# Starting the form of 64 steps at unit 8 instead of unit 12 in an RWKV attention fused with a SwiGLU feed-forward

## The chip, the cores and the metric

The kernel runs on one core of a Trainium2 chip. A core has five engines with instruction streams of their own: TensorE (PE: matmuls, with weight loads shown as PEld), VectorE (DVE), ScalarE (ACT), GpSimd (POOL) and SyncE (SP), which here does nothing but issue DMAs. Each engine works through its stream in the order in which the program emits it, and semaphores make one engine wait for another. The metric is the device time of one execution in microseconds (us), as the median of several runs.

## The reference

A linear attention with a per-channel decay, over 4 batches, 8 heads, 768 steps and 48 channels a head, is followed by a SwiGLU feed-forward over its 3072 x 384 output:

```python
for t in range(S):
    kt, vt, rt = (k[:, :, t], v[:, :, t], r[:, :, t])
    cur = np.einsum('bhd,bhe->bhde', u[None] * kt, vt)
    y[:, :, t] = np.einsum('bhd,bhde->bhe', rt, state + cur)
    state = w[None, :, :, None] * state + np.einsum('bhd,bhe->bhde', kt, vt)
...
g = x @ w_gate                       # x: y as (3072, 384), w_gate: (384, 1536)
val = x @ w_val
return (g / (1 + np.exp(-g)) * val @ w_out)
```

## The kernel before

**Units.** The attention is cut into 24 units. A unit below `PAIRED` is 128 steps of one batch. A unit from `PAIRED` on is 64 steps of two batches: one batch in partitions 0 to 63, the other in 64 to 127 (`part`, `pieces_of`). The decay is folded into the keys and receptances (`scale_k`, `scale_r`, on GpSimd), so that inside a unit only a masked product is left.

**What a unit goes through.**

- `load` and `load_v` bring k, r and v in by SP's queue: three kinds of transfer, where a unit of two batches needs twice as many DMAs of half the size.
- `scale_k`, `scale_r`, and `own_product` (r times k times u, for the step's own term; `own_sum` adds it up on VectorE, `diagonal` lets ScalarE write it out as diagonal matrices).
- The turn, which puts channels on partitions. Below `BLOCKS` TensorE does it (`turn`: eight transposes by matmul, then two copies on ScalarE). From `BLOCKS` on, SP moves 32-wide blocks into one fixed pair of tiles (`move_blocks`: four DMAs, or eight for a unit of two batches) and VectorE transposes these 32 x 32 blocks (`turn_block` n = 0 for the keys, 1 for the receptances).
- `scores` (keys by receptances) and a masked copy of the scores into `At` on VectorE. For a unit of two batches, `fill_turned` (SP) and `fill_own` (ScalarE's queue) put the turned receptances and the diagonals into the other halves of `At`.
- `outputs` (TensorE; ScalarE copies the result into `xT`), and `update` or `paired_update` of the state (TensorE, VectorE, GpSimd). The last updates before `PAIRED` copy the state into the free half of `v_ld` by SP.

**The stages.** The loop over `s` is the pipeline. In stage `s` unit `s + 1` is scaled, unit `s` is turned, the scores of unit `s - 1` and the outputs of unit `s - 2` are computed. From `LATE` on, the outputs and the update of unit `s - 2` stand right behind the scores instead of at the end of the stage. Between these parts stand up to five gaps (`gaps(s, n)`). In stages 4 to 11 the table `EARLY` says what fills a gap: `R` is one step of the weights (`round_weights`, or later `weight_sum`), `F` is one `feed`.

**The weights.** The feed-forward's weights come as 64-bit numbers in 18 chunks: 0 to 11 for gate and value, 12 to 17 for the output matrix. One `R` rounds chunk n on ScalarE (`round_high`, `round_low`, `round_high`) and VectorE (`round_dve`), adds the low part of chunk n - 1 on GpSimd, and lets SP load chunk n + 2 (`load_weights`, into three buffers `w_bits`). In stage 7 chunks 10, 11 and 12 are rounded and 12, 13 and 14 loaded; in stage 8 chunks 13, 14 and 15 are rounded and 15, 16 and 17 loaded; in stage 9 chunks 16 and 17 are rounded.

**feed.** One `feed` takes the next item of the feed-forward from `todo` (for example `gate_value`: 12 matmul records into one of two PSUM banks, a Silu on ScalarE, a product on VectorE that gives the bank back), then one deferred piece of the attention's VectorE work from `lazy`, then one to three diagonals from `small`. `after_visit(s)`, in stages from `PAIRED` on, writes down the order of `lazy`: masked copies, `own_term` (`own_sum` and `diagonal` of the next unit), `turn_block(s, 0)`, a masked copy, `turn_second`, a masked copy, and the sums of the state. `turn_second` is more than VectorE's work:

```python
def turn_second():
    turn_block(s, 1)
    fill_turned(s)
    if s + 1 < N:
        scale_r(s + 1)
        move_blocks(s + 1)
        if s + 3 < N:
            load(s + 3)
```

What is left in `lazy` and `small` at the start of the next stage's scores is emitted there. From stage 12 on, a formula spreads the items left in `todo` over the gaps.

Of the kernel before, what the change touches and what calls it, by code (L numbers as in the profile page):

```python
# [22 lines left out]
def fast(  # L23
# [31 lines left out]
    N = B * NCH  # L55
# [64 lines left out]
    def rhat_of(i):  # L120
        return rhat[i % 2 if i < BLOCKS else i % 4 // 2]

# [3 lines left out]
            return khat[i][:, :, 0:D], rhat[i % 2][:, :, 0:D]  # L126
        return k_ld[i % 2][:], r_ld[i % 2][:]

    PAIRED = 12

    def part(i, p):

        c, q = divmod(i - PAIRED, 2)
        return 2 * q + p, PAIRED // B * P + 64 * c

    def pieces_of(i):

        if i < PAIRED:
            c, b = divmod(i, B)
# [3 lines left out]
    def load(i):  # L143
        for src, dst in zip((k, r), raw(i)):
            for rows, b, t in pieces_of(i):
                n = rows.stop - rows.start
                sp.dma_start(out=dst[rows], in_=src[b, :, t : t + n, :].rearrange("h t d -> t h d"))  # L147
# [106 lines left out]
    def round_weights():  # L254
        if done["act"] > done["pool"]:
            round_pool()
        round_act()
# [15 lines left out]
    def own_sum(i):  # L273
        dus[i] = three.tile([P, H], FP32, name="du", tag="du")
        dve.tensor_reduce(dus[i][:], rks.pop(i), axis=AX.X, op=ALU.add)
# [51 lines left out]
    for l in range(7):  # L327
        n = 1 << l
# [15 lines left out]
    def at(i, a):  # L344

        return HP - 1 - a if i >= BLOCKS and i % 2 else a

# [7 lines left out]
    def scale_r(i):  # L355
        pool.tensor_mul(rhat_of(i)[:, :, 0:D], raw(i)[1], rscale)
# [14 lines left out]
    def diagonal(i, on_act=None):  # L371

        du = dus.pop(i)
        if i >= PAIRED:
            small.extend(
                lambda h=h: act.activation(  # L376
                    own[:, i % 2, slot(i, h), :], ident64, AF.Identity, scale=du[:, h : h + 1]
                )
                for h in range(H)
            )  # L380
            return
        on_act = on_act or (HP if i < 4 else H)
        small.extend(
            lambda h=h: act.activation(
                At[i % 2][:, h, :], ident[:], AF.Identity, scale=du[:, h : h + 1]
            )
            for h in range(on_act)
        )
        if on_act < H:
            n = H - on_act  # L390
            pool.tensor_mul(
                At[i % 2][:, on_act:H], ident[:].unsqueeze(1).to_broadcast([P, n, P]),
                du[:, on_act:H].unsqueeze(2).to_broadcast([P, n, P]),
            )
# [16 lines left out]
    def move_blocks(i):  # L411


        h = hats[:].rearrange("p n h x -> p (n h x)")
        first, step = ((0, 1), (11, -1), (12, 1), (23, -1))[i % 4]
        if i < PAIRED:
            for m in range(4):
                src = h[:, P * first + 32 * m : P * first + 32 * m + 1]
                sp.dma_start(
                    out=h[32 * m : 32 * m + 32, 24 * P : 32 * P],  # L420
                    in_=bass.AP(
                        tensor=src.tensor, offset=src.offset,
                        ap=[list(src.ap[0]), [P * step, 2 * HP], [1, 32]],
                    ),
                )
            return
        first = 2 * first + (step < 0)
        for p in range(2):
            for n in range(2):
                for m in range(2):  # L430
                    q, o = 64 * p + 32 * n, 64 * first + 32 * m
                    src = h[q : q + 32, o : o + 1]
                    q, o = 64 * (1 - p) + 32 * m, 63 * 64 + 32 * n
                    dst = h[q : q + 32, o : o + 1]
                    sp.dma_start(
                        out=bass.AP(
                            tensor=dst.tensor, offset=dst.offset,
                            ap=[list(dst.ap[0]), [-64, 2 * H], [1, 32]],
                        ),
                        in_=bass.AP(  # L440
                            tensor=src.tensor, offset=src.offset,
                            ap=[list(src.ap[0]), [64 * step, 2 * H], [1, 32]],
                        ),
                    )

    def turn_block(i, n):

        if n == 0:
            turned[i] = three.tile([P, HP, P], FP32, name="rT", tag="rT")
        dst = (kT[i % 2], turned[i])[n]  # L450
        if i < PAIRED:
            merged = hats[:, 6:8].rearrange("p n h x -> p (n h x)").rearrange(
                "p (q n a x) -> p n q a x", q=4, n=2, a=HP
            )
            dve.transpose(dst[:].rearrange("p a (t q) -> p q a t", q=4), merged[:, n])
        else:
            dve.transpose(dst[:].rearrange("p a t -> p (a t)"), blocks[n])

    def after_visit(s):
# [10 lines that stand above are left out]
        def own_term():  # L470
            own_sum(s + 1)
            diagonal(s + 1)

        masked, sums = list(lazy)[:4], list(lazy)[4:]
        if len(masked) < 4:
            masked = [*masked, *(lambda: None for _ in range(4 - len(masked)))]
        lazy.clear()
        lazy.extend([
            *masked[:2], own_term if s + 1 < N else lambda: None,
            lambda: turn_block(s, 0), masked[2], turn_second, masked[3], *sums,  # L480
        ])

    lazy = deque()

    def scores(i):
# [20 lines left out]
        lazy.popleft()()  # L506
        if i < BLOCKS:
            lazy.popleft()()
# [10 lines left out]
    def fill_turned(i):  # L519

        rT = turned[i][:].rearrange("p a (e t) -> p (a e) t", e=2)
        for p in range(2):
            there = slice(64 - 64 * p, P - 64 * p)
            sp.dma_start(out=both(i)[there, p], in_=rT[there])
# [187 lines left out]
    def weight_sum():  # L712

        n = len(summed)
        o = (wt[1][:], w12, wt[0][:], wt[2][:])[n]
        a, b = ((w22, w12), (w12, w11), (w22, w12), (w21, wt[0][:]))[n]
        pool.tensor_sub(o, a, b)
        summed.append(n)
# [584 lines left out]
    summed = []  # L1303
    todo = []

    def feed(n, pops=1):
        for _ in range(n):
            ready = [k for k, (need, _) in enumerate(todo) if need <= done["pool"] + len(summed)]
            if ready:
                todo.pop(ready[0])[1]()  # L1310
            for _ in range(min(len(lazy), 1 + (len(lazy) > 9))):
                lazy.popleft()()
            for _ in range(min(pops, len(small))):
                small.popleft()()
# [22 lines left out]
    def gaps(s, n):  # L1337

        if s not in EARLY:
            if n == 0:  # L1340
                coming = 40 * ((s < 14) + (s < 18)) + 14 * (s < 22)
                share[0] = -(-(len(todo) + coming) // max(25 - s, 1))
            feed(
                share[0] // 5 + (n < share[0] % 5) - (n == 1 and BLOCKS <= s < PAIRED),
                1,
            )
            return
        for what in EARLY[s][n]:
            if what == "R":
                if done["pool"] < NW:  # L1350
                    round_weights()
                elif len(summed) < 4:
                    weight_sum()
            else:
                feed(1, 3)

    share = [0]
    BLOCKS = 10
    LATE = 12
    EARLY = {s: ("" if s < 7 else "R", "F", "R", "F", "RF") for s in range(5, 12)}  # L1360
    EARLY[4] = ("R", "F", "", "F", "F")

# [87 lines left out]
    for s in range(4, N + 2):  # L1450
        if 4 < s <= PAIRED:
            own_sum(s)
        if s == PAIRED:
            diagonal(s)
        late = BLOCKS < s + 1 < N and s % 2 == 0
        if s + 3 == PAIRED:

            for e in range(2):
# [3 lines left out]
                sp.dma_start(out=w64[rows, :, 1 - e], in_=w64[o : o + 64, :, 1 - e])  # L1462
        if s + 1 == BLOCKS:
            turn(s)
# [14 lines left out]
        if 4 <= s - 1 < N:  # L1479
            flush()  # L1480
            while lazy:
                lazy.popleft()()
            if s - 2 >= PAIRED:
                outputs(s - 2)
                if s < N:
                    fill_own(s)
            scores(s - 1)
            if LATE <= s < PAIRED + 2:
                outputs(s - 2)
                update(s - 2)  # L1490
                fill_own(s)
            if PAIRED <= s < N:
                load_v(s)
                after_visit(s)
            gaps(s, 1)
# [14 lines left out]
        gaps(s, 2)  # L1510
        if 4 <= s - 2 < LATE - 2:
            outputs(s - 2)
# [35 lines left out]
    n = nc.values_load(outside, min_val=0, max_val=512)  # L1548
# [416 lines left out]
```

## Time and profile before

| | |
|---|---|
| median of 3 runs | 581.66 us (581.47 to 581.78) |
| profiled execution | 582.02 us, its span 580.2 us |
| mean granted TensorE clock | 0.999 |
| DMA | 48.09 MB in 151734 packets, of them 139313 under 512 B |
| stage 8, from the scores of unit 7 to those of unit 8 | 74.80 to 86.95 us |
| stage 14, from the scores of unit 13 to those of unit 14 | 177.24 to 201.10 us |

The span runs from the first to the last instruction; the time of an execution lies a little around it. In the lines of the profile a row of the chain or of a timeline gives the start, the length, the engine, what it writes or the line of the kernel, and how many instructions are merged (x8). SPq and ACTq are the DMAs that SP and ACT issue. TensorE's fp32 matmuls show as two records each. The lines of the kernel that matter here: L405 the turn by TensorE, L494 scores of a 128-step unit, L645 its outputs, L658 its update; L546, L580 and L594 the same three for a unit of two batches; L688 `gate_value`; L204 and L210 the rounding on ACT; L219 and L220 on VectorE; L252 the addition on GpSimd; L184 the loading of a chunk; L147 `load`; L153 `load_v`; L419 and L435 `move_blocks`; L457 `turn_block`; L524 `fill_turned`; L530 `fill_own`; L675 the copies of the state; L384 and L376 the diagonals.

### The profile page before, as it was taken

The page shows a single profiled execution, that of the slowest core. Times are in us where ns is not written, and L with a number is a line of the kernel's source. Part 1 is how long each engine was busy: PE and PEld are TensorE (multiplying, and loading weights), DVE is VectorE, ACT ScalarE, POOL GpSimd, SP SyncE. Part 2 cuts the span into 40 slices and gives each one's busy share as a digit, 9 for nine tenths or more (in the row PEclk, how much of TensorE's full clock was granted, in tenths as well). Part 3 has the DMA queues.
Part 4 walks back from the last instruction along what each step waited for, and adds up shares of the span by engine and source line. Part 5 has one row for each costly group of instructions (what it writes and reads, how often), then busy time and mean ns, then how long its engine had stood idle before and what let it go on. Part 6 is the DMA issues. An engine that isn't in the chain of part 4 may idle for free.

```text
span 580.2 us, 13566 instructions
## 1 busy us (share of the span) xinstructions
PE 569.1 (98%) x5370; PEld 514.0 (89%) x5370; DVE 427.9 (74%) x746; ACT 224.6 (39%) x532; POOL 391.5 (67%) x394
## 2 busy tenths in 40 slices
PE   7989999999999999999999999999999999999996
PEld 6778888899888899988899988899988899988896
DVE  6978877388497689597879597869268787477672
ACT  3759787341344422353521344430233320233310
POOL 6789888989999727979527979528988950010610
PEclk9999999999999999999999999999999999999999
DMA  7989985652626515644425643310200000200002
GB/s 189 241 238 249 265 261 84 80 86 54 136 41 99 91 28 115 130 71 80 75 41 92 134 79 68 54 35 21 55 0 1 1 0 2 55 0 2 2 1 58
DMA packets 151734, 48.09 MB, mean 83 GB/s; under 512 B 139313, under 2 KB 142386, under 8 KB 151666
## 3 DMA queue, kind: packets, MB, share of 16 engines
q1 hardware_dynamic: 147218, 40.69, 33.5%
q10 hardware_dynamic: 4448, 6.49, 4.1%
q8 instruction: 43, 0.70, 0.5%
q14 instruction: 25, 0.20, 0.1%
HBM read 28.31 MB, written 4.72 MB: 57 GB/s over the span
## 4 chain that ended last, share of the span: by engine, by line
PE 95%; DMA 1%; DVE 1%; SPq 1%; issue 0%; ACT 0%; DVEq 0%
PE bank L957 32%; PE bank L768 19%; PE ring L957 13%; PE bank L688 11%; PE bank L1190 8%; PE ring L645 3%; PE ring L580 2%; PE ring L494 2%; PE ring L546 1%; DMA v_ld<-in_v_dram 1%; PE ring L1190 1%; PE ring L405 1%; PE ring L594 1%; PE ring L658 1%; SPq L147 0%
## 5 line engine op out<-in xcount | busy, mean ns | idle before, releaser
L981 DVE TENSOR_TENSOR hv<-hv,bank 128x512 f32<-128x512 f32 x132 | 87.9, 683 | 38.5 <-PE bank L957 32.5
L688 PE MATMUL bank<-xT,wgv 128*128 128x256 f32 x288 | 66.3, 384 | 0.0
L957 PE MATMUL bank<-xf,wgv 128*128 128x256 f32 x256 | 65.7, 381 | 0.0
L981 ACT COPY hv<-bank 128x512 f32<-128x512 f32 x72 | 40.8, 584 | 57.6 <-PE bank L957 51.8
L688 PEld LDWEIGHTS bank<-xT,wgv 128*128 128x128 f32 x288 | 53.4, 190 | 8.2 <-POOL wgv L228 0.2
L957 PEld LDWEIGHTS bank<-xf,wgv 128*128 128x128 f32 x256 | 48.0, 190 | 6.8 <-DVE kT L1235 0.6
L1244 POOL TENSOR_TENSOR hv<-At,hats 128x512 f32<-128x512 f32 x8 | 10.2, 1274 | 63.7 <-ACT At L1243 63.7
L988 ACT ACTIVATE hv<-hv 128x512 f32<-128x512 f32 (+2 forms) x36 | 22.7, 633 | 48.6 <-DVE hv L981 42.3
L376 ACT ACTIVATE zs<-mask,du 128x64 f32<-128x64 f32 x96 | 29.8, 346 | 19.8 <-DVE hv L781 9.3
L957 PE MATMUL bank<-xT,wgv 128*128 128x256 f32 x144 | 35.5, 379 | 0.0
L957 PE MATMUL bank<-xT,s 128*128 128x256 f32 x152 | 35.2, 380 | 0.0
L768 PE MATMUL bank<-wt,hs 128*128 128x192 f32 x192 | 34.1, 328 | 0.0
L768 PE MATMUL bank<-wo,hs 128*128 128x192 f32 x192 | 33.8, 326 | 0.0
L745 POOL TENSOR_TENSOR hs<-hv,hs 128x768 f32<-128x768 f32 x6 | 11.3, 1878 | 32.2 <-DVE hs L742 32.2
L768 PE MATMUL bank<-wo,hv 128*128 128x192 f32 x192 | 32.8, 327 | 0.0
L887 POOL TENSOR_TENSOR s<-s,wgv 128x256 f32<-128x256 f32 x39 | 30.6, 784 | 2.9
L957 PEld LDWEIGHTS bank<-xT,s 128*128 128x128 f32 x152 | 28.7, 190 | 4.2 <-issue 0.2
L887 POOL TENSOR_TENSOR s<-s 128x256 f32<-128x256 f32 x39 | 31.4, 805 | 0.9
L768 PEld LDWEIGHTS bank<-wo,hv 128*128 128x128 f32 x192 | 31.6, 190 | 0.4
L768 PEld LDWEIGHTS bank<-wo,hs 128*128 128x128 f32 x192 | 31.7, 190 | 0.2
L768 PEld LDWEIGHTS bank<-wt,hs 128*128 128x128 f32 x192 | 31.4, 190 | 0.2
L887 POOL TENSOR_TENSOR s<-wgv 128x256 f32<-128x256 f32 x39 | 29.7, 781 | 2.1 <-PE bank L768 2.1
(239 smaller groups left out, 1438.5 us busy)
## 6 DMA issues: line engine op xcount, KB each, us to landing
hats<-hats SPq DMA_DIRECT2D x96, 64.0 KB, 2.4
w_bits<-in_moe_w_gate_dram SPq DMA_DIRECT2D x6, 768.0 KB, 6.3
w_bits<-in_moe_w_val_dram SPq DMA_DIRECT2D x6, 768.0 KB, 6.4
w_bits<-in_moe_w_out_dram SPq DMA_DIRECT2D x6, 768.0 KB, 6.8
At<-zs ACTq DMA_DIRECT2D x24, 128.0 KB, 3.8
At<-rT SPq DMA_DIRECT2D x24, 128.0 KB, 2.3
v_ld<-in_v_dram SPq DMA_DIRECT2D x24, 96.0 KB, 6.2
k_ld<-in_k_dram SPq DMA_DIRECT2D x24, 96.0 KB, 3.6
```

The source lines that it names most:

```text
L376: lambda h=h: act.activation(own[:, i % 2, slot(i, h), :], ident64, AF.Identity, scale=du[:, h : h + 1])
L494: pe.matmul(ps[e][:, a, :], kT[i % 2][rows, at(i, a), :], turned[i][rows, at(i, a), :], start=True, stop=True, skip_group_check=True,)
L580: pe.matmul(ps[32 * q : 32 * q + 32, cc, 64 * p : 64 * p + 64], *x, start=start, stop=stop, skip_group_check=True,)
L645: pe.matmul(ps[32 * q : 32 * q + 32, cc, :], *x, start=start, stop=stop, skip_group_check=True,)
L688: pe.matmul(gv[:, o, :].rearrange("p (i t) -> p i t", i=2), wt[:, c, P * f : P * (f + 1)], xT[:, 2 * g % NX : 2 * g % NX + 2, c, :], start ...
L745: on.tensor_sub(s[1], h12, x["s"][1])
L768: pe.matmul(ps, lhs[:, f, :], rhs[:, f, :], start=(f == 0 and n in (0, 1, 4)), stop=(f == FH - 1), skip_group_check=True,)
L887: op(made[o], made[a], made[b])
L957: pe.matmul(ps[:, o], u[:, o], v, start=first and o == 0, stop=True, skip_group_check=True,)
L981: do(out, *(pair_of(wide[a][:]) if isinstance(a, str) else a for a in args))
L988: todo.append((at, lambda: act.activation(gate, gate, AF.Silu)))
L1190: pe.matmul(ps, (h[what][q] if h[what] is D_ else h[what][:, q])[:, f, :], wide["o"][what][:, f, :], start=first and f == 0 and (split or ...
```

## The change

The form of two batches begins at unit 8 (`PAIRED`), and so does the turn by VectorE (`BLOCKS`) and the place of outputs and update right behind the scores (`LATE`). Units 8 to 23 now cover steps 256 to 767 in pieces of 64. In the first stage of the new form, the diagonals of the next unit (`own_term`) come last in `lazy`, and in the last stage `own_term` is left out. In the gaps of stages 4 to 11 a feed takes up to four pieces from `lazy` instead of one.

```diff
-    PAIRED = 12
+    PAIRED = 8
...
-            *masked[:2], own_term if s + 1 < N else lambda: None,
+            *masked[:2], own_term if PAIRED < s < N - 1 else lambda: None,
             lambda: turn_block(s, 0), masked[2], turn_second, masked[3], *sums,
         ])
+        if s == PAIRED:
+            lazy.append(own_term)
...
-    def feed(n, pops=1):
+    def feed(n, pops=1, lazies=1):
         for _ in range(n):
...
-            for _ in range(min(len(lazy), 1 + (len(lazy) > 9))):
+            for _ in range(min(len(lazy), lazies + (len(lazy) > 9))):
                 lazy.popleft()()
...
             else:
-                feed(1, 3)
+                feed(1, 3, 4)
...
-    BLOCKS = 10
-    LATE = 12
+    BLOCKS = 8
+    LATE = 8
```

In the order of SP's queue this puts `move_blocks(8)` between the loads of chunks 12 and 13 in stage 7, and in stage 8 the state copies of unit 6 and `load_v(8)` ahead of chunk 16, and `fill_turned(8)`, `move_blocks(9)` and `load(11)` ahead of chunk 17.

## The prediction

> **What bounds the kernel now.** I read the page first: busy shares, then the chain that ended last.
>
> ```profile
> PE 569.1 (98%) x5370; PEld 514.0 (89%) x5370; DVE 427.9 (74%) x746; ACT 224.6 (39%) x532; POOL 391.5 (67%) x394
> PE 95%; DMA 1%; DVE 1%; SPq 1%; issue 0%; ACT 0%; DVEq 0%
> ```
>
> TensorE has work in 98% of the span and carries 95% of the chain. So a microsecond of matmuls removed is a microsecond of time, as long as TensorE is never made to wait; a microsecond of new waiting is lost for good, since no later stage has slack on TensorE to win it back.
>
> The chain in order of time gives TensorE's price of one stage of each form: first stage 8 of before (loop index s = 8, with unit 7's scores), then the attention pieces of a stage in the 64-step form, then, from the groups of instructions, how often TensorE turns keys and receptances.
>
> ```profile
> 73.93 0.87 PE ring L405 x8
> 74.80 1.09 PE ring L494 x16
> 75.89 2.79 PE bank L688 x12
> 78.68 1.68 PE ring L645 x56
> 80.36 0.34 PE ring L658 x32
> 80.70 5.38 PE bank L688 x24
> ...
> 176.20 1.04 PE ring L580 x64
> 177.24 0.62 PE ring L546 x32
> 177.87 0.45 PE ring L594 x32
> ```
>
> ```profile
> L405 PE MATMUL ring<-ident,hats 128*128 128x128 f32 x80 | 11.4, 289 | 0.0
> ```
>
> A 128-step unit costs 0.87 (turn, L405) + 1.09 (scores) + 1.68 (outputs) + 0.34 (update) = 3.98 us; without the turn 3.11. A 64-step unit costs 1.04 + 0.62 + 0.45 = 2.11. The 80 turns of eight per unit are units 0 to 9, so today units 8 and 9 pay 3.98 and units 10 and 11 pay 3.11. Between attention pieces stand the items of the feed-forward, 2.69 us each (5.38 for two), three to a stage here.
>
> Next I asked what the other engines and the DMA do in those stages.
>
> ```profile
> 74.80:86.95 12.15, 12.15 (x151) 10.54 (x150) 9.84 (x21) 9.95 (x24) 10.38 (x10) 1.00 0.78 241
> 177.24:201.10 23.86, 23.86 (x233) 20.85 (x232) 18.34 (x32) 11.44 (x26) 20.23 (x23) 1.00 0.52 88
> ```
>
> Columns: PE, PEld, DVE, ACT, POOL, granted clock, DMA share, GB/s. Stage 8 is only 12.15 us long, and in it all three vector engines work 10 us and the DMA engines are 78% busy, because the feed-forward weights still come in. A stage of the 64-step form today is 24 us long, with no weights. The change puts four stages of that form into the short, crowded place.
>
> **The change: what it takes away.** Units 8 and 9: 2 x (3.98 - 2.11) = 3.74 us. Units 10 and 11: 2 x (3.11 - 2.11) = 2.00. Together **-5.74 us** of TensorE. Items of the feed-forward are conserved: the two extra feeds between VectorE's turns in stages 10 and 11 go, and the items are shared out later. ACT loses two copies per turn for units 8 and 9; no TensorE time hangs on these.
>
> **What it adds: SP's queue.** Each 64-step stage issues load_v x4, fill_turned x2, move_blocks x8 and load x4 from SP, which issues in order.
>
> ```profile
> 64.96 0.37 SPq L147 DMA_DIRECT2D k_ld<-in_k_dram  x1
> ...
> 66.04 3.59 SPq L184 DMA_DIRECT2D w_bits<-in_moe_w_out_dram  x3
> ```
>
> ```profile
> 191.12 1.16 SPq L524 DMA_DIRECT2D At<-rT  x2
> 192.37 5.42 SPq L435 DMA_DIRECT2D hats<-hats  x8
> 197.84 1.35 SPq L147 DMA_DIRECT2D k_ld<-in_k_dram  x2
> 199.23 1.32 SPq L147 DMA_DIRECT2D r_ld<-in_r_dram  x2
> 204.56 3.02 SPq L153 DMA_DIRECT2D v_ld<-in_v_dram  x4
> ```
>
> That is 1.16 + 5.42 + 2.67 + 3.02 = 12.3 us of issuing per stage, against 3 x 2.69 + 2.11 = 10.2 us of TensorE. In a 24 us stage this is hidden; in a 10 us stage it isn't. Worse, the last six weight chunks (12 to 17, out weights) are loaded from the same queue in stages 7 and 8. Today these three-packs leave SP with nothing but loads before them. In the new order chunk 13 is issued behind move_blocks(8), chunk 16 behind the state copies of update(6) and load_v(8), and chunk 17 behind fill_turned(8), move_blocks(9) and load(11). How long chunks and blocks take to land:
>
> ```profile
> L184 SPq DMA_DIRECT2D w_bits<-in_moe_w_out_dram x6: 368/414/727, 66.0 to 81.4; - x6
> ...
> DMA to landing us min/median/max: 6.0/6.8/7.7
> ```
>
> ```profile
> hats<-hats SPq DMA_DIRECT2D x96, 64.0 KB, 2.4
> ```
>
> I take 6.0 for a chunk (it no longer travels behind others of its kind) and 2.4 for blocks. When ACT wants the chunks, and what it has behind them:
>
> ```profile
> 76.33 0.54 ACT L204 ACTIVATE bank<-w_bits 128x384 f32<-128x384 f32 x1
> ...
> 78.03 0.69 ACT L384 ACTIVATE At<-ident,du 128x128 f32<-128x128 f32 x2
> ...
> 128.32 2.02 ACT L376 ACTIVATE zs<-mask,du 128x64 f32<-128x64 f32 x8 [1.40 <-DMA v_ld<-zs]
> 132.71 0.48 ACT L649 COPY xT<-ring 128x384 f32<-128x384 f32 x1 [2.37 <-PE ring L645]
> 132.72 1.28 ACTq L530 DMA_DIRECT2D At<-zs  x2
> ```
>
> ```profile
> L694 ACT ACTIVATE sgs<-bank x15: 358/384/386, 62.1 to 116.0; 128x256 f32<-128x256 f32 x15
> L220 DVE SCALAR_TENSOR_TENSOR wo<-bank,wo x12: 556/557/558, 73.7 to 95.7; 128x384 int32<-128x384 int32 x12
> L695 DVE TENSOR_TENSOR hv<-sgs,bank x16: 394/421/422, 59.6 to 116.4; 128x256 f32<-128x256 f32 x16
> L457 DVE STREAM_TRANSPOSE rT<-hats x6: 698/704/711, 146.3 to 255.3; 128x512 f32<-128x512 f32 x6
> L554 DVE COPY_PREDICATED At<-mask,ring x20: 428/444/454, 157.8 to 256.4; 64x256 f32<-64x256 int32 x20
> ```
>
> **First wait, chunk 13.** load(10) is now four DMAs: SP is at 64.96 + 2.67 = 67.6, chunk 12 to 68.0, move_blocks(8) to 73.5, so chunk 13 lands at about 79.5. ACT wants it today at 76.33. ACT, in order, holds behind it: the chunk's three rounding steps (76.33 to 78.03, 1.7 us), 0.69 of diagonals, unit 8's eight diagonals 2.02, the copy of xT 0.48, the issue of fill_own 1.28, and the Silu 0.38 = 6.55 us. Only then VectorE multiplies (0.42) and frees one of the two gate banks; it turns block 0 (0.70) and rounds chunk 14 (four operations of 0.56, 2.2), multiplies (0.42), turns block 1 (0.70): 79.5 + 11.0 = 90.5. TensorE is free for unit 8's scores at 73.93 + 1.09 + 2.02 + 8.07 = 85.1. Wait: **5.4 us**. Bounds: 2.2 where the chunk is in time (76.33 + 11.0 = 87.3), 7.1 where it lands at 7.7. The row nearest is the landing of out chunks itself, so I take 5.4.
>
> **Second wait, chunk 17.** Count from the end of block 1's turn, t0 (90.5). SP then issues fill_turned 1.16, move_blocks(9) 5.42, load(11) 2.67: 9.3 us, and chunk 17 lands at t0 + 15.3. VectorE rounds it and only behind that turns unit 9's second block: 2.9 (rounding from the first L204 on) + 0.42 + 0.44 + 0.70 = 4.4, so unit 9's scores start at t0 + 19.7. TensorE comes there after 0.62 + 2.02 + 8.07 + 1.04 = 11.75. Wait: **7.9 us**. Bounds: 9.6 with a landing of 7.7; 1.3 if the chunk cost nothing, since then move_blocks(9) lands at t0 + 9.0 and VectorE still turns twice, rounds and multiplies (about 4 us) before the scores.
>
> **Third wait, the loop of the blocks.** One pair of block tiles serves all units: move_blocks(10) can't start before unit 9's second block is turned. From there 1.16 + 5.42 + 2.4 = 9.0, then turn, masked copy, multiply, turn, masked copy = 0.70 + 0.44 + 0.42 + 0.70 + 0.44 = 2.7, so outputs of unit 9 can start 11.7 us after its scores, where TensorE is there after 0.62 + 0.45 + 8.07 = 9.1. Wait: **2.5 us** (0 to 5, the upper end with blocks that take twice 2.4 to land). In stage 12 the items ahead of the scores cover the next turn.
>
> GpSimd's additions, the four small copies on ACT and the earlier copies of w64 and the scales move with the change and lie beside TensorE's work; I cost them at nothing, up to 1 us if GpSimd, 10.38 of 12.15 us busy, is late with the state of unit 6, which SP waits for ahead of load_v(8).
>
> **Sum.** -5.74 + 5.4 + 7.9 + 2.5 = +10.1 us on the profiled execution (582.02 us with a span of 580.2, some 0.4 above the median of 581.66). Both large waits have more room below than above, so I take +9.3 rather than the whole: 581.66 + 9.3 = **591 us**. Its own range: with the lower ends -5.7 + 2.2 + 1.3 = -2.2 us, 579.5; with the upper ends -5.7 + 7.1 + 9.6 + 5 = +16, 598.
>
> **The rivals.**
>
> - *No wait at all* (faster). If what I call SP's issuing is overlapped, or the three engines' backlog drains inside the stages, only -5.74 remains: **576 us**. For it: in stage 8 TensorE is busy for all 12.15 us although three other engines are over 80% busy, so there is slack in the buffers that I can't see. Against it: SP's 12.3 us exceed 10.2. It decides where chunk 17 lands before t0 + 6. Chance 0.14.
> - *Half of the waits.* Chunk 13 in time (2.2), the wait for chunk 17 at half of its size (4), none for the loop: -5.7 + 6.2, about 582, from 579 to 585. Chance 0.14, split 0.05 faster, 0.05 same, 0.04 slower.
> - *A clock that falls in the gaps.* The forecast puts two waits of over 4 us into a TensorE that works through 98% of its span today, with a granted clock of 1.00 in both quoted stages. If it halved for one item after each, 2 x 2.69 = 5.4 us more: **596 us**. Chance 0.12. The Trainium skill, "TensorE: Matmul & The Clock Gate", section "Part 1: The HAM clock gate", says that an idle window of about 3.4 us drops the clock to half until about 3.4 us of work have passed. By it, as an estimate, two gaps cost 2 x 1.7 = 3.4 us, and the sum would be 594 to 595; the trace, with TensorE busy throughout those stages, can't show it.
> - *My forecast.* 0.60.
>
> So faster by over 0.2% (which is about what a measurement of this kernel tells from no change): 0.14 + 0.05 = 0.19; same 0.05; slower 0.04 + 0.12 + 0.60 = 0.76. The range from 580 to 598 leaves out the no-wait case and part of the half case below, and little above.
>
> **What would show each step.** In the profile after: attention pieces of units 8 to 11 in the chain at 1.04, 0.62 and 0.45, with no L405 after 70 us (the gain). Waits of ACT L204 on a w_bits DMA near 76 to 80 us and again at the last two chunks (first and second wait). SP's w_bits spread out between move_blocks instead of in three-packs. Idle time of TensorE before L546 released by VectorE's L457, twice (second and third). Busy shares of TensorE from 75 to 125 us below 90%. I am wrong in the mechanism if ACT doesn't wait for w_bits at all, and wrong in size if the waits for chunks 13 and 17 together are under 6 us.

## The result and the profile after

The changed kernel takes 608.35 us (median of 4 runs, 606.34 to 611.6), beside 581.72 us for the kernel before: a ratio of 1.0463 with a 95% interval from 1.0428 to 1.0498. The profiled execution has a span of 606.9 us against 580.2, so 26.7 us are to be found. Of all runs in this document one is left out of its median and ratio, a run of the last kernel below that took 598.52 us at a granted clock of 0.948, where the other seven had 0.990 to 0.995. Lines after 481 of the kernel before carry numbers larger by two: L690 is `gate_value`'s matmul, L548, L582 and L596 are scores, outputs and update of a unit of two batches, L697 is VectorE's gate product, L770 a projection item.

The page of after, busy shares, clock by slices of 15.2 us, and the chain that ended last:

```profile
PE 571.4 (94%) x5450; PEld 513.8 (85%) x5450; DVE 434.1 (72%) x766; ACT 221.2 (36%) x528; POOL 393.2 (65%) x394
...
PEclk9999978599999999999999999999999999999999
...
PE 75%; DMA 7%; POOL 7%; SPq 3%; DVE 2%; issue 2%; ACT 2%; POOLq 0%; DVEq 0%; ACTq 0%
```

TensorE's share of the chain fell from 95% to 75%. The rest went to DMA, GpSimd, SP, VectorE and ScalarE, and the clock row shows 7, 8 and 5 in the slices from 76 to 121 us. TensorE's rows in order of time (start, duration, operation; in brackets the idle time ahead and what ended it) put the loss in its places:

```profile
88.68 5.49 PE L690 MATMUL bank<-xT,wgv 128*128 128x256 f32 x12 [6.87 <-DVE hv L697]
94.10 0.89 PE L548 MATMUL ring<-rT,kT 48*64 48x64 f32 x32
...
116.46 1.72 PE L582 MATMUL ring<-At,v_ld 128*32 128x64 f32 x56 [11.24 <-DVE At L556]
118.11 1.13 PE L548 MATMUL ring<-rT,kT 48*64 48x64 f32 x32
119.02 1.05 PE L596 MATMUL ring<-v_ld,hats 64*64 64x48 f32 x32
120.00 8.95 PE L690 MATMUL bank<-xT,wgv 128*128 128x256 f32 x36
128.88 1.28 PE L582 MATMUL ring<-At,v_ld 112*32 112x64 f32 x64
...
131.23 0.62 PE L548 MATMUL ring<-rT,kT 48*64 48x64 f32 x26 [0.82 <-DVE v_ld L612]
...
141.35 4.17 PE L770 MATMUL bank<-wo,hv 128*128 128x192 f32 x24 [1.66 <-DVE hv L697]
149.57 3.67 PE L770 MATMUL bank<-wt,hs 128*128 128x192 f32 x12 [4.06 <-DVE hs L744]
153.18 1.11 PE L582 MATMUL ring<-At,v_ld 112*32 112x64 f32 x64
...
155.29 2.22 PE L770 MATMUL bank<-wo,hv 128*128 128x192 f32 x12
...
194.42 2.16 PE L959 MATMUL bank<-xf,s 128*128 128x256 f32 x8 [1.19 <-ACT hv L983]
```

- **The gain is there.** Where nothing disturbs it, a unit of two batches runs from 153.18 to 155.29: 2.11 us, as forecast.
- **Waits:** 6.87 + 11.24 + 0.82 + 1.66 + 4.06 + 1.19 = 25.8 us.
- **Slow matmuls** behind the long waits, from start to start. Twelve L690 take 88.68 to 94.10, 5.42 for the usual 2.69: 2.7. The last outputs, scores and update take 116.46 to 120.00, 3.54 for 1.98 (2.11 less the 8 outputs done before the wait): 1.6. Three items take 120.00 to 128.88, 8.88 for 8.07: 0.8. The item at 149.57 takes 3.61 to the outputs at 153.18, beside 1.95 for one of its kind: 1.7. Together 6.8.

So -5.7 + 25.8 + 6.8 = 26.9 us, beside 26.7 measured. What the two large waits hang on shows in ScalarE's rows, where the rounding of a weight chunk (L204) waits for its DMA (chunks 13, 16 and 17 here), and in SP's:

```profile
82.30 0.51 ACT L204 ACTIVATE bank<-w_bits 128x384 f32<-128x384 f32 x1 [4.61 <-DMA w_bits<-in_moe_w_out_dram]
...
87.79 0.38 ACT L696 ACTIVATE sgs<-bank 128x256 f32<-128x256 f32 x1 [0.89 <-ACT xT L651]
...
97.50 0.54 ACT L204 ACTIVATE bank<-w_bits 128x384 f32<-128x384 f32 x1 [1.18 <-DMA w_bits<-in_moe_w_out_dram]
...
111.50 0.51 ACT L204 ACTIVATE bank<-w_bits 128x384 f32<-128x384 f32 x1 [7.50 <-DMA w_bits<-in_moe_w_out_dram]
```

```profile
68.54 1.33 SPq L184 DMA_DIRECT2D w_bits<-in_moe_w_out_dram  x1
69.91 6.27 SPq L435 DMA_DIRECT2D hats<-hats  x8
76.28 1.59 SPq L184 DMA_DIRECT2D w_bits<-in_moe_w_out_dram  x1
...
92.36 1.15 SPq L526 DMA_DIRECT2D At<-rT  x2
93.60 7.14 SPq L435 DMA_DIRECT2D hats<-hats  x8
100.79 2.60 SPq L147 DMA_DIRECT2D k_ld<-in_k_dram  x2
103.44 1.31 SPq L147 DMA_DIRECT2D r_ld<-in_r_dram  x2
104.85 0.57 SPq L184 DMA_DIRECT2D w_bits<-in_moe_w_out_dram  x1
...
117.22 7.63 SPq L435 DMA_DIRECT2D hats<-hats  x8
```

Chunk 13 leaves SP at 76.28, behind the eight block moves of unit 8, and ScalarE has it at 82.30. The Silu behind it comes at 87.79, and VectorE's product frees the gate bank for TensorE at 88.68. Chunk 17 leaves SP at 104.85, behind `fill_turned`, the moves of unit 9 and `load`, and ScalarE has it at 111.50. Then come VectorE's rounding, its turn and its masked copies, and TensorE goes on at 116.46. Between the two the chain of waits that ended last, in order of time, runs from one chunk to the next:

```profile
76.28 5.93 DMA w_bits<-in_moe_w_out_dram
...
85.11 1.32 DVE At L504 x2
...
87.31 0.52 POOL zs L673
...
91.50 5.92 DMA w_bits<-in_moe_w_out_dram
...
104.85 6.63 DMA w_bits<-in_moe_w_out_dram
```

The late chunk 13 holds VectorE's masked copies, these the state's product on GpSimd, and SP, which must copy that state, stands still (its next DMAs leave at 87.27) with `load_v(8)` and chunk 16 behind. So lateness comes back into the queue that made it. SP is therefore not busy throughout: nothing leaves it from 80.44 to 87.27, and again from 109.61 to 115.96, where `fill_turned` waits for VectorE.

### The profile page after: what moved, and what is told of

Its sections match the earlier page's. It is cut to its first block, busy times and chain, and to the rows that moved or that the text cites. A ratio compares the mean times of both kernels' runs of the same rounds, so it can differ in the third digit from the quotient of the medians.

```text
span 606.9 us, 13839 instructions
## 1 busy us (share of the span) xinstructions
PE 571.4 (94%) x5450; PEld 513.8 (85%) x5450; DVE 434.1 (72%) x766; ACT 221.2 (36%) x528; POOL 393.2 (65%) x394
## 4 chain that ended last, share of the span: by engine, by line
PE 75%; DMA 7%; POOL 7%; SPq 3%; DVE 2%; issue 2%; ACT 2%; POOLq 0%; DVEq 0%; ACTq 0%
PE bank L959 28%; PE bank L770 14%; PE ring L959 13%; PE bank L1192 8%; PE bank L690 5%; DMA w_bits<-in_moe_w_out_dram 4%; POOL wgv L862 3%; PE ring L582 3%; POOL s L889 2%; PE ring L548 1%; DMA v_ld<-in_v_dram 1%; PE ring L1192 1%; PE ring L647 1%; DMA w_bits<-in_moe_w_val_dram 1%; PE ring L596 1%
## 5 line engine op out<-in xcount | busy, mean ns | idle before, releaser
L690 PE MATMUL bank<-xT,wgv 128*128 128x256 f32 x288 | 69.3, 398 | 6.9 <-DVE hv L697 6.9
L690 PEld LDWEIGHTS bank<-xT,wgv 128*128 128x128 f32 x288 | 55.8, 198 | 16.1 <-DVE hv L697 7.3
L983 ACT COPY hv<-bank 128x512 f32<-128x512 f32 x72 | 40.8, 585 | 61.8 <-PE bank L959 54.4
L376 ACT ACTIVATE zs<-mask,du 128x64 f32<-128x64 f32 x128 | 38.8, 345 | 26.4 <-DVE du L275 10.4
L770 PE MATMUL bank<-wt,hs 128*128 128x192 f32 x192 | 35.5, 338 | 4.1 <-DVE hs L744 4.1
L615 POOL TENSOR_TENSOR v_ld<-v_ld,w 48x384 f32<-48x384 f32 x28 | 24.4, 871 | 19.1 <-DVE v_ld L612 16.0
L770 PEld LDWEIGHTS bank<-wt,hs 128*128 128x128 f32 x192 | 32.9, 197 | 4.5 <-POOL rk L267 4.3
L959 PE MATMUL bank<-xT,wgv 128*128 128x256 f32 x144 | 35.6, 380 | 0.0
L770 PE MATMUL bank<-wo,hv 128*128 128x192 f32 x192 | 32.9, 327 | 1.7 <-DVE hv L697 1.7
L770 PE MATMUL bank<-wo,hs 128*128 128x192 f32 x192 | 34.0, 327 | 0.0
L770 PEld LDWEIGHTS bank<-wo,hv 128*128 128x128 f32 x192 | 31.5, 190 | 2.4 <-DVE hv L697 2.0
```

The source lines that it names most:

```text
L376: lambda h=h: act.activation(own[:, i % 2, slot(i, h), :], ident64, AF.Identity, scale=du[:, h : h + 1])
L615: pool.tensor_mul(ze, ze, w.unsqueeze(3).to_broadcast([D, HP, 2, D]))
L690: pe.matmul(gv[:, o, :].rearrange("p (i t) -> p i t", i=2), wt[:, c, P * f : P * (f + 1)], xT[:, 2 * g % NX : 2 * g % NX + 2, c, :], start ...
L770: pe.matmul(ps, lhs[:, f, :], rhs[:, f, :], start=(f == 0 and n in (0, 1, 4)), stop=(f == FH - 1), skip_group_check=True,)
L959: pe.matmul(ps[:, o], u[:, o], v, start=first and o == 0, stop=True, skip_group_check=True,)
L983: do(out, *(pair_of(wide[a][:]) if isinstance(a, str) else a for a in args))
```

## The experiments

All ratios are to the kernel before, with 95% intervals. Two theories stood at the start: **late chunks** (theory A of the expectations: only the order in which the weight chunks leave SP is at fault) and **the queue** (SP has more to issue in these stages than they have time for, whatever comes first). A third, **the clock**, puts part of the loss on slow matmuls.

**The chunks on another queue.** Chunks 10 to 17 leave from ScalarE's queue, ahead of the rounding of the chunk two earlier.

```diff
-            sp.dma_start(
+            (act if n >= 10 else sp).dma_start(
...
     def round_first(n):
+        if n >= 8:
+            load_weights()
...
-        load_weights()
+        if n < 8:
+            load_weights()
```

> The changed kernel, but chunks 10 to 17 of the weights are loaded from ScalarE's queue, each at the start of the rounding step two chunks earlier, so they no longer stand behind block moves and state copies on SP. Theory A (late chunks hold ScalarE, and through it VectorE and TensorE): ScalarE's waits for w_bits in stages 8 and 9 (4.6, 1.2, 7.5 us in the changed kernel) shrink to under 1 us each, TensorE's waits of 6.9 and 11.2 us fall to under 3 us each, and the time to 584 to 592 us. Rival B (the chain of block moves, turns and fills doesn't fit the short stages, whatever the weights do): TensorE's long waits stay within 2 us of what they are, time over 600 us.

603.66 us, ratio 1.0376 (1.0349 to 1.0402). ScalarE's waits for chunks are gone, and TensorE's wait ahead of unit 8's outputs falls from 11.24 to 4.47, but the first wait grows from 6.87 to 7.98. The first row is ScalarE's, the diagonals of unit 8; the second TensorE's, in the same kernel:

```profile
87.57 2.02 ACT L379 ACTIVATE zs<-mask,du 128x64 f32<-128x64 f32 x8 [5.01 <-DMA v_ld<-zs]
```

```profile
91.74 4.71 PE L693 MATMUL bank<-xT,wgv 128*128 128x256 f32 x12 [7.98 <-DVE hv L700]
```

Now ScalarE waits 5.01 us for the next thing in SP's queue, the state copies of unit 5 behind the moves of unit 8. Late chunks alone fall as a theory: another transfer takes their place. It isn't only the order on SP, either. One of the block moves ahead of those copies took 8.12 us to land, by the chain of the same kernel, where the median of such moves in before is 2.4:

```profile
78.80 8.12 DMA hats<-hats
```

So slow transfers are a rival to slow issuing, and no run here parts the two. In after itself chunks 13, 16 and 17 reach ScalarE 6.0 to 6.65 us after they leave SP, no later than the 6.0 to 7.7 of before; there the chunks' delay lies in leaving late.

**The block moves alone.** Two kernels start from before. One moves only `BLOCKS`, so that units 8 and 9 are turned by VectorE in the 128-step form. The other only adds unused moves, eight in stage 7 and eight in stage 8.

```diff
-    BLOCKS = 10
+    BLOCKS = 8
```

> The kernel before with only the turn by VectorE beginning at unit 8; the form of two batches still begins at 12. Saves two turns by TensorE, 1.7 us. Four block DMAs per unit in place of eight, no fills. Theory A: the chunks are late here too, by 4 to 6 us, as the same queue carries them behind the moves of units 8 and 9; ScalarE waits for w_bits for 2 to 6 us in stages 8 and 9; time 582 to 590 us. Rival B: no long wait, time 579.5 to 582 us.

```diff
...
+        if s == 7:
+            extra_moves(8)
         gaps(s, 2)
+        if s == 8:
+            extra_moves(8)
```

> The kernel before with eight more block DMAs on SP in stage 7 (ahead of chunk 13) and eight in stage 8 (behind chunk 16, ahead of chunk 17), into the block tiles, which nothing reads before they are overwritten; nothing else is changed. It measures the cost of the queue alone. Theory A: ScalarE waits 2 to 4 us for chunk 13 and 1 to 3 us for chunk 17; of that 1 to 4 us reach the end, time 582.5 to 586 us. Rival B: no change, 581.2 to 582.2 us.

The first took 594.51 us, 1.0218 (1.0195 to 1.0242), although it takes 1.74 us off TensorE (two turns of 0.87). The second took 586.27 us, 1.0091 (1.0057 to 1.0124), with nothing but sixteen more DMAs on SP. ScalarE's rows of the first, then of the second:

```profile
81.41 0.54 ACT L204 ACTIVATE bank<-w_bits 128x384 f32<-128x384 f32 x1 [5.57 <-DMA w_bits<-in_moe_w_out_dram]
...
101.94 0.54 ACT L204 ACTIVATE bank<-w_bits 128x384 f32<-128x384 f32 x1 [5.63 <-DMA w_bits<-in_moe_w_out_dram]
```

```profile
78.50 0.54 ACT L204 ACTIVATE bank<-w_bits 128x384 f32<-128x384 f32 x1 [2.80 <-DMA w_bits<-in_moe_w_out_dram]
...
96.87 0.52 ACT L204 ACTIVATE bank<-w_bits 128x384 f32<-128x384 f32 x1 [3.16 <-DMA w_bits<-in_moe_w_out_dram]
```

Moves on SP in these stages make the chunks late, whether anyone needs the moves or not. In the first kernel TensorE waits 3.75 and 3.21 us behind them. In the second the buffers take up most of that: TensorE's longest wait in these stages is 1.39, in the profile of the quickest of its four runs (583.47). The first kernel, with half as many moves of twice the size, loses far more than the second. There VectorE has to turn what the moves bring, and SP stands still from 76.88 to 88.21, with chunks 16 and 17 behind the moves of unit 9, until VectorE has turned unit 8.

**The queue relieved, in after.** One kernel leaves out the loads of chunks 12 to 17, one the block moves of units 8 to 11, one both.

```diff
...
+            if n >= 12:
+                bits[n] = kept[0]
+                return
...
```

> The changed kernel without the loads of chunks 12 to 17: their rounding reads chunk 11 again, so the output matrix holds other values; all instructions but these six DMAs are there. Theory A (late chunks, and their traffic ahead of other small transfers): TensorE's first two waits (6.9 and 11.2 us) shrink to under 3 us together with their cold clock, time 582 to 590 us. Rival B (the chain of moves, turns and fills): at least 10 us of waits remain in stages 8 to 11, time over 596 us.

```diff
...
+        if i < 12:
+            return
```

> The changed kernel without the block moves of units 8 to 11 (32 DMAs): VectorE turns zeros or old blocks there, so the values of these units are others. Theory A in its form 'block moves in SP's queue hold up everything behind them': chunks are in time, no wait of TensorE over 2 us in stages 8 to 11, time 576 to 584 us. Rival C (the new order of VectorE's and ScalarE's own work, with diagonals, fills and outputs early in the stage, is what holds TensorE): waits of over 8 us remain, time over 590 us.

> Both edits of the two runs before at once: the changed kernel without the loads of chunks 12 to 17 (rounding reads chunk 11 again) and without the block moves of units 8 to 11 (VectorE turns zeros or old blocks); the output holds other values. If late chunks and block moves were two separate causes that add up (10 and 14 us), the time is 583 to 586 us. If they are one cause, the same queue, seen twice, the time stays at 591 to 595 us, and what remains is the engines' own work in short stages, stage 12, and the clock.

They take 598.07 us, 1.0274 (1.0251 to 1.0297), without the chunks; 594.51, 1.022 (1.0203 to 1.0237), without the moves; 593.7, 1.0203 (1.0186 to 1.022), without both. From 608.35 that is 10.3, 13.8 and 14.7 us. Without the moves TensorE's waits in stages 8 to 11 are 2.15 at most, and still the time is far above 584. The two parts don't add up. Two sides of one full queue would do that; so would a floor at some 594 us that other hand-offs set, and the waits that stay speak for such a floor too. Without both, TensorE's long waits are these, by its rows in order of time:

```profile
102.38 1.72 PE L591 MATMUL ring<-At,v_ld 128*32 128x64 f32 x56 [3.84 <-DVE At L565]
...
132.96 4.18 PE L779 MATMUL bank<-wt,hs 128*128 128x192 f32 x12 [4.06 <-DVE hs L753]
```

**The items left over.** The changed stages 10 and 11 have one feed fewer each. Put back, in after and then in the kernel without chunks and moves:

```diff
+    EARLY[10] = EARLY[11] = ("R", "F", "RF", "F", "RF")
```

> The changed kernel with one more item of the feed-forward in each of stages 10 and 11, where the kernel before had one between VectorE's two turns. If the waits in stage 12 (1.7, 4.1 and 1.2 us) come from items that are left over and meet sums that VectorE makes late, they shrink by 3 us or more and the time is 2 to 6 us under the changed kernel's, 602 to 606 us. If they come from VectorE being behind as such, no change.

> The run without chunks 12 to 17 and without the moves of units 8 to 11, and with one more item in each of stages 10 and 11. If stage 12's waits come from left-over items, they go here as well and the time is 3 to 5 us under the run without this edit; TensorE's waits after 125 us are then under 2 us together. If VectorE is behind as such, they stay at 5 us or more.

In after: 605.38 us, 1.0416 (1.0381 to 1.045); 3.0 us less, with intervals that overlap. In the relieved kernel: 588.68, 1.0113 (1.0096 to 1.013), 5.0 us less, with intervals apart. In the relieved kernel the wait for `h_sums` falls from 4.06 to 1.99, and one of 1.85 comes later; under 2 together was expected. Not all of the gain is items that no longer stand behind one another. VectorE's first addition of `h_sums` takes 3.48 or 3.49 us in six of the seven kernels that have after's feeds, 0.95 in the one with one lazy piece per feed (below), and 0.96 in all four with the feeds put back. From its start to TensorE's next matmul it is 5.29 us in after and 2.61 in the relieved kernel with the feeds.

**The clock.** 45 dummy matmuls ahead of unit 8's outputs keep TensorE at work through most of the wait of 11.24.

```diff
+                if s == 10:
+                    warm(45, ring_a[2])
                 outputs(s - 2)
```

> The changed kernel with 45 more 128x128 matmuls on TensorE ahead of the outputs of unit 8 (stage 10), where it waits 11.2 us; their result is never read. They take about 10 us and lie in the wait. Clock rival: the granted clock stays near 1 through that wait (0.5 to 0.6 without them), the matmuls behind it run at full speed, time 2 to 3 us shorter than the changed kernel. Without a part for the clock: the same time or longer.

TensorE's rows of this kernel in order of time:

```profile
115.52 1.00 PE L582 MATMUL ring<-At,v_ld 128*32 128x64 f32 x56 [1.14 <-DVE At L556]
116.45 0.69 PE L548 MATMUL ring<-rT,kT 48*64 48x64 f32 x32
116.96 0.63 PE L596 MATMUL ring<-v_ld,hats 64*64 64x48 f32 x32
```

The outputs, scores and update now take 1.00, 0.69 and 0.63 instead of 1.72, 1.13 and 1.05, so the clock held; the time is 610.06 us, 1.0496 (1.0473 to 1.0518), no better than after. At this gap the slow matmuls cost nothing that reached the end: TensorE was going to wait for others again, 1.00 us ahead of the next outputs, where after has no wait, and 2.55 instead of 1.66 ahead of the projection. The other gaps were not tried.

**Two other orders.** One lazy piece per feed, as before, instead of up to four; and chunk 13 ahead of the moves of unit 8, chunks 16 and 17 ahead of those of unit 9, with the feeds put back.

```diff
-                feed(1, 3, 4)
+                feed(1, 3)
```

> The changed kernel with one deferred piece per feed in stages 4 to 11, as before: block moves are then mostly emitted at the start of the next stage, behind all chunk loads of stage 8. Theory A: ScalarE's waits for chunks 16 and 17 go, but unit 9's scores wait for their turn in its place; time 598 to 612 us. Rival D (taking four pieces at once is what puts the moves ahead of the chunks and costs the time): under 592 us.

```diff
+    EARLY[8] = ("R", "F", "RR", "F", "F")
+    EARLY[10] = EARLY[11] = ("R", "F", "RF", "F", "RF")
...
-        if BLOCKS <= s + 1 <= PAIRED:
-            move_blocks(s + 1)
-            if s + 1 < PAIRED:
-                load_v(s + 1)
...
+        if s + 1 == PAIRED:
+            move_blocks(s + 1)
```

> The changed kernel, whole, with SP's order mended: move_blocks(8) behind chunk 13 and the state copies of unit 5, both rounding steps of stage 8's second half ahead of turn_second, so that chunks 16 and 17 go ahead of fill_turned(8) and move_blocks(9), and one more item in each of stages 10 and 11. If the order in the queue is the cause, ScalarE's waits for chunks fall under 2 us each and the time to 592 to 599 us; if the queue is simply too full, whatever its order, over 601 us. The kernel before is not expected to be reached.

The first is no different from after: 609.67 us, 1.0484 (1.0457 to 1.0511). The wait for chunk 17 goes, but unit 8's scores wait 6.40 for VectorE's turn. The second gets 8.8 us back, of which the feeds alone had given 3.0: 599.57 us, 1.0314 (1.0285 to 1.0343). Its scores of unit 8 then wait 7.15 us for VectorE's turn. It isn't the moves that are late for that turn. VectorE does it at 92.28, behind the rounding of chunks 14 and 15, and these chunks now leave SP behind unit 8's moves, so that ScalarE waits for chunk 14. ScalarE's row, then TensorE's:

```profile
86.50 0.51 ACT L204 ACTIVATE bank<-w_bits 128x384 f32<-128x384 f32 x1 [3.97 <-DMA w_bits<-in_moe_w_out_dram]
```

```profile
93.04 1.14 PE L548 MATMUL ring<-rT,kT 48*64 48x64 f32 x32 [7.15 <-DVE rT L457]
```

ScalarE's waits were expected under 2 us each, and the time lies between the two forecasts. The order can be better; this one makes chunk 14 late in place of 13 and 17.

**What stays without the queue's load.** In the kernel without chunks and moves and with the feeds put back, TensorE still waited 3.84 us ahead of unit 8's last outputs while VectorE was hardly idle. This kernel takes VectorE's rounding of chunks 12 to 17 out as well.

```diff
...
         hi = mags.pop((n, half))
         f = hi.shape[2]
+        if n >= 12:
+            return
...
-            pool.tensor_tensor(dst, dst, low, ALU.add)
+            pool.tensor_tensor(dst, low if n >= 12 else dst, low, ALU.add)
...
```

> The kernel of g2_and_feeds (no loads of chunks 12 to 17, no block moves of units 8 to 11, two more feeds) and also without VectorE's rounding of chunks 12 to 17: four operations of 0.56 us a chunk, 2.24 us, leave VectorE, while ScalarE's and GpSimd's work on these chunks stays. In g2_and_feeds TensorE still waits 3.84 us ahead of unit 8's last outputs (101.48), for a masked copy of VectorE, and VectorE is hardly idle from 88.0 to 101.9. Theory VectorE's own load: the wait of 3.84 goes to under 0.5 and the 9 matmul groups behind it run at the full clock (another 2 to 2.5 us), so the ratio to before goes from 1.0113 to 1.000 to 1.005 (582 to 585 us). Rival, ScalarE's rounding steps or its issue of fill_own set that wait: it stays over 2 us and the time over 586.

585.73 us, 1.0069 (1.0045 to 1.0093). VectorE's rows in this kernel, then TensorE's:

```profile
88.59 0.42 DVE L708 TENSOR_TENSOR hv<-sgs,bank 128x256 f32<-128x256 f32 x1 [2.93 <-ACT sgs L707]
...
93.04 0.42 DVE L708 TENSOR_TENSOR hv<-sgs,bank 128x256 f32<-128x256 f32 x1 [3.38 <-ACT sgs L707]
```

```profile
99.72 1.46 PE L593 MATMUL ring<-At,v_ld 128*32 128x64 f32 x56 [3.10 <-DVE At L567]
...
126.57 3.41 PE L781 MATMUL bank<-wt,hs 128*128 128x192 f32 x12 [1.97 <-DVE hs L755]
```

VectorE's own load was the wrong reading of that wait, although the kernel is 2.95 us quicker without it. VectorE is now idle for about 3 us at a time, and TensorE still waits 3.10. VectorE waits for ScalarE's Silu, which stands in ScalarE's order behind the rounding of chunks. By the trace a chain of hand-offs between two engines that work in order sets the pace. That the rounding on ScalarE is what makes it long was not tried.

No version beat the kernel before.

## Why the prediction was right in direction and too small

The forecast was +9.3, and the account of the trace came to +26.9. Of the 17.6 between them, the idle time of the first wait is 1.5 more than its term, that of the second 3.3 more and that of the third 1.7 less. The waits of stage 12 and the one at 194 us, which stood at nothing, are 6.9, the slow matmuls 6.8, and 0.8 had been taken off the sum. So three steps failed: the size of the second wait, the items of stages 10 and 11 at no cost, and the clock as a rival outside the sum.

- **The gain, -5.74:** right. A piece of two batches costs 2.11 us where it runs undisturbed, and the turns on TensorE end at 61.8:

```profile
L405 PE MATMUL ring<-ident,hats x64: 272/273/421, 6.5 to 61.8; 128*128 128x128 f32 x64
```

- **First wait, chunk 13, 5.4:** right in mechanism, and 6.87 measured, within the bounds. Chunk 13 reached ScalarE at 82.30 instead of 79.5, because the moves took 6.27 us to issue, not 5.42, chunk 12 ahead of them took 1.33, and the loads before that ended 0.9 later than I had them. But the wait sits one step earlier than I wrote: ahead of an item, for the gate bank (L697), not ahead of the scores for a turn. And it is followed by 2.7 us of slow matmuls, so that the scores came 9.7 us late, which is above the upper bound of 7.1.

- **Second wait, chunk 17, 7.9:** mis-sized. 11.24 of idle, and the scores of unit 9 came 12.3 us late. They start 24.01 us after those of unit 8 (94.10 to 118.11), where TensorE's own work is 11.75. From the end of VectorE's turn (t0 = 92.3, just ahead of SP's row at 92.36) the chunk was issued at t0 + 12.5, not t0 + 9.3: moves of 7.14 us instead of 5.42, loads of 3.9 instead of 2.67, and small gaps between them. It came to ScalarE 6.65 us after its issue, not 6.0, so at t0 + 19.2 and not t0 + 15.3. The issue prices had come from rows in a 24 us stage with no weights in flight. Besides, the working let the outputs of unit 8 run ahead of the wait; but 56 of these 64 wait for the last masked copy, so their 1.65 us come behind it.

- **Third wait, the loop of the blocks, 2.5:** not seen as such. Stage 10 did lose 2.6: from 118.11 to 130.08 it took 11.97 us for 10.18 of work (0.62 + 0.45 + 8.07 + 1.04), the difference all of it slow matmuls, and then TensorE waited 0.82 for a sum of VectorE (L612). The size agreed for another reason.

- **"In stage 12 the items ahead of the scores cover the next turn"** and "the items are shared out later", at no cost: wrong. Stage 12 lost 1.66 + 4.06 of idle and 1.7 of slow clock, 7.4 us. Items that fell out of stages 10 and 11 stood behind one another, and the projection waited for VectorE's `h_sums`, where one addition took 3.49 us instead of 0.96. With the feeds back stage 12 cost 3 to 5 us less, and that addition was short again. Why it is long without them is open (below).

- **The clock** was a rival at 0.12 and should have been a term of the sum. The prediction had two waits of over 4 us in its own working, and the trace has 6.8 us of slow matmuls. The Trainium skill, "TensorE: Matmul & The Clock Gate", section "Part 1: The HAM clock gate", has the clock fall to half after an idle window of about 3.4 us and come back after one such window of work or more. The waits of 4.06, 6.87 and 11.24 agree (the granted clock is 0.50 from 88 to 94 us, all along the 5.42 us of the first twelve matmuls), and so do the 1.19 and 1.66, behind which the granted clock stayed at 1.00. The 1.97 of the last kernel, followed by 3.41 us for twelve projection matmuls that take 2.11, doesn't, and there the measurement stands. By the run with dummy matmuls one gap's share cost nothing at the end, so the 6.8 is an account of the trace, not what a steady clock would bring back.

- **GpSimd and small copies, 0 to 1:** SP did wait for GpSimd's product of unit 6's state ahead of `load_v(8)`, the place I had named, but not because GpSimd was full: its input was late, behind chunk 13, as the chain shows. I had the queue feed the waits and not the waits feed the queue; ScalarE's wait for chunk 16, 1.18 us, comes of it.

- **Taking 9.3 of the sum's 10.1** because "both large waits have more room below than above" was wrong: each late transfer delayed the next, and the errors added upward. The waits that I had bounded one by one share that queue, and the range, made of separate bounds, ended at 598.

The theory of the queue holds in part: moves alone cost time (sixteen unused DMAs, 0.9%), and either half of the load taken away gives back 10 to 14 us, both together hardly more. What in that load costs the time is not settled. These runs take away the issuing on SP and the transfers at once, and the profile's DMA share in after is 0.73 from 74 to 94 us and 0.64 from 94 to 118, beside 0.78 in stage 8 and 0.52 in stage 14 of before. And SP stood still for 6.8 and 6.35 us, held up by engines that were late themselves.

The loss to be explained is 32.4 us: 26.6 in time and 5.74 of TensorE's work that is gone. SP's two loads are worth 14.7 of it, the feeds put back 5.0, and VectorE's rounding of these chunks 2.95, measured one on top of the other. The last kernel, at 585.73, still has about 9.8 us of the loss. Its profile has waits of 3.10 and 1.97, some 3 us of slow matmuls behind them, and a mean granted clock of 0.992; no run removes these.

## What to carry to other kernels

A form that saves time on the busiest engine but needs more, smaller DMAs fits only into stages longer than its queue's issuing, its landing and the hand-offs behind it; add these up for the stage into which it moves, with issue times taken under that stage's traffic. Look for what else leaves from the same queue in that phase: a late weight chunk holds ScalarE, then VectorE, then the TensorE whose time was saved. When an edit takes filler work out of a stage, ask what the next stages do with it before costing it at nothing.

## What the hardware showed that I had not expected

- Issuing eight block moves took SP 5.42 us in the 24 us stage of before, and 6.27, 7.14 and 7.63 us in the stages of after, while other transfers were in flight. In the kernel with the chunks first it was 8.15 us, by SP's row:

```profile
94.26 8.15 SPq L435 DMA_DIRECT2D hats<-hats  x8
```

- VectorE's first addition of `h_sums` in stage 12 took 3.49 us, where seven others of the kernel like it took 0.95 to 1.27, and in before the same one took 0.97. It is no accident of one run: six kernels show 3.48 or 3.49 in that place, as said above. GpSimd worked without a pause beside it; whether that was the cause was not tried. The one in after, and the one of before:

```profile
144.28 3.49 DVE L742 TENSOR_TENSOR hs<-hv 128x768 f32<-128x768 f32 x1
```

```profile
120.80 0.97 DVE L740 TENSOR_TENSOR hs<-hv 128x768 f32<-128x768 f32 x1
```

- The clock can fall behind a wait of only 1.97 us (or of 1.90 in the first kernel with moves alone, followed by 3.39 us for twelve matmuls), and need not behind one of 1.99: the relieved kernel with its feeds back waits that long at the same place and runs on at 2.19 us for the twelve matmuls, by TensorE's row:

```profile
129.52 2.19 PE L779 MATMUL bank<-wt,hs 128*128 128x192 f32 x12 [1.99 <-DVE hs L753]
```
